# Scores of batch 2 in the fixed PSUM banks, a changed load order, and four softmax products on VectorE, in a fused attention and ELU block

## The chip, the cores and the metric

The kernel runs on one core of one Trainium2 chip. The metric is the device time of one execution in microseconds (us); the number given for a kernel is the median of several runs. Beside it one execution was profiled, and every duration of a single instruction comes from that execution.

## What is computed

For each of 8 batches a small attention block reads x (8 heads, 512 rows, 64 columns) against a state (8 heads, 32 rows, 64 columns), in both directions. The result, 512 + 32 rows of 512 columns per batch, goes through a two-layer block with ELU:

```python
scores = scale * x @ state.T;   a  = softmax(scores);   xread = a @ state
scores2 = scale * state @ x.T;  a2 = softmax(scores2);  sread = a2 @ x
h = concat([xread, sread], rows) @ w_in          # (4352, 512) @ (512, 2048)
g = where(h > 0, h, exp(min(h, 0)) - 1)          # ELU
out = g @ w_out                                  # (4352, 2048) @ (2048, 512)
```

The two weight matrices arrive as 64-bit floating point numbers, which the kernel itself turns into 32-bit ones.

## The kernel before, in words

**Algebra.** xread @ w_in = a @ (state @ w_in), so the kernel first makes M = state @ w_in for each batch (`make_m`) and then multiplies the softmax by M (`ffn1`). From batch 2 on, and for the second layer of all batches, it uses a Strassen-like scheme with seven products for eight, partly on two levels (class `Second`). That takes sums and differences of blocks, of activations and of weights, nearly all on VectorE (`sums`, `weights`, `combine`, `weight_sum`, `sum_a`), and those of M on GpSimd (`sum_m`).

**The stages.** `start` (L1150) does batches 0 and 1 together with the preparation of the weights. w_in and w_out come in 16 blocks of 1 MB (`weight_block`, L1117): blocks 0 to 7 are w_in, 8 to 15 w_out. Block 0 comes in two halves. `convert` (L1090) makes 32-bit numbers of a block by two passes on ScalarE and four on VectorE: a clamp (`tensor_scalar`), a combination (`scalar_tensor_tensor`), a shift (`tensor_scalar`) and an add, which the trace shows as a custom instruction. Three raw buffers (tile t_w) hold blocks in flight, and block n + 3 is asked for when block n is converted. Each converted block of w_in feeds `make_m` for both batches and goes back to memory (w_in_mem), where later batches fetch it. Still within `start`, the second layer of batch 0 runs (n0), and that of batch 1 (n1) begins. `ffn2_1` (L1364) finishes batch 1, on the way making the weight sums of the second level. Then the loop runs `batch(b)` for batches 2 to 7, and `states` ends with the rows of the states.

**Softmax.** `scores` (L662) writes one product into two PSUM banks. `softmax` (L760) then does, for the two halves g: a transpose from PSUM (VectorE), the maximum of 32 (VectorE), its subtraction (GpSimd), exp (ScalarE), the sum (VectorE); then a scalar step on ScalarE and a reciprocal on VectorE for both halves; then, for each half, the product with the reciprocal (L779) and a transpose into the tile that the matmuls read. The buffers are in the tile sec for batches 0 and 1 and in xr for later ones. `softmax_rows` (L746) works on the same scores for the other direction. Later `sum_a` takes four differences of the result of `softmax`.

**What sets the order.** All operations go to a planner (class `Plan`, L87), not straight to the engines. The planner knows each operation's inputs and outputs and an estimated cost, and runs a list scheduling over all of them when the program is built. TensorE takes its operations by their place in the program text, and passes over one that isn't ready or has no PSUM bank; VectorE, ScalarE and SP take the one that is due first; GpSimd keeps the order of the text. The result is a fixed order of instructions on each engine; on the chip each engine runs its own order and waits where it must. For the first 40 us of the plan idle time of TensorE is filled with matmuls whose result nobody reads (`fill`, L1587, traced as line 1590).

**PSUM banks.** There are 8. Most are given out by the planner: the one that came free first goes to the next operation that opens one, and its last user gives it back. Banks 6 and 7 are taken for good at one point (`fixed`, L559) and serve as the accumulator pb of `ffn1_chunk` from batch 2 on. Before that point they are given out like the others. In the kernel before, the point is `ident_ready` (L1137, called at L1580 and L1581 between `start` and `ffn2_1`): for each of the two banks, four 128x128 matmuls of w_out with itself, made to follow the last TensorE operation of `start`. The dictionary `kept` (L208) names, for the operation that first uses a fixed bank, that bank. `scores(2, xr)` (L1260), inside `start`, takes two ordinary banks; the scores of batches 3 to 7 (L1303) go to the fixed banks.

**Loads at the start** (L1172 to L1181), in this order by rank: the state of batch 0 (queues of SP and ScalarE), x of batch 0 in four transfers (alternately SP and ScalarE), block 0 in two (SP), the state of batch 1 (SP), x of batch 1 in four (SP), blocks 1 and 2 (SP). An x transfer moves 256-byte pieces, a block 2048-byte ones.

In the trace nearly all instructions have line 464, the one that issues every planned operation, so they are told apart by their tiles: o, s and sec for outputs and sums, t_w for raw blocks and later for weight sums, w_half and w_out for converted weights, aT for the softmax, m for M. An fp32 matmul shows as two records.

Of the kernel before, what the change touches and what calls it, by code (L numbers as in the profile page):

```python
# [86 lines left out]
class Plan:  # L87
# [108 lines left out]
    def prepare(self):  # L196
        for op in self.ops:
            op.users = []
            op.turn = self.places.get(op.number, op.number)
        for op in self.ops:  # L200
            for d in op.deps:
                d.users.append(op)
        self.opening = {}
        self.closing = {}
        for b in self.banks:
            self.opening.setdefault(b.first, []).append(b)
            self.closing.setdefault(b.last, []).append(b)
        self.kept = {b.first: b.fixed for b in self.fixed}  # L208
        self.all_banks = min([op.number for op in self.kept], default=0)

    def lag(self, a, b):
# [27 lines left out]
    def run(self, until=0.0):  # L239
# [6 lines left out]
        able = {e: [] for e in ENGINES}  # L246
        coming = {e: [] for e in ENGINES}
        banks = [(0.0, i) for i in range(self.BANKS)]
        fixed = set(self.kept.values())
        openers = sorted((op for op in self.ops if op in self.opening), key=lambda op: op.turn)  # L250
        oldest, opened = 0, set()
        in_turn = [op for op in self.ops if op.engine == POOL]
# [6 lines left out]
        def bank_time(op):  # L259

            if op in self.kept:
                return min([t for t, i in banks if i == self.kept[op]], default=None)
            need = len(self.opening[op])
            if op is not openers[oldest] and op.number > self.all_banks:
                need += self.KEPT_BANKS
            free = choice(op)
            return free[need - 1][0] if need <= len(free) else None
# [40 lines left out]
        while len(done) < len(self.ops):  # L308
# [24 lines left out]
                    after.append((holder[i], op))  # L333
                opened.add(op)
            if op in self.kept:
                banks = [b for b in banks if b[1] != self.kept[op]]
                if self.kept[op] in holder:
                    after.append((holder[self.kept[op]], op))
            while oldest < len(openers) and openers[oldest] in opened:
                oldest += 1  # L340
            if e == PE and (op.spare or op.name == "make_m"):
# [48 lines left out]
def kernel(  # L390
# [16 lines left out]
    G = 2  # L407
# [266 lines left out]
    def make_m(b, *hcs):  # L674
# [11 lines left out]
        if hcs[-1] % 2 == 0:  # L686
            plan.ops[-1].spare = st[b, "m", c][0].bank

    def m_blocks(m):
        return [m[:, g * 512 + h * 256 : g * 512 + (h + 1) * 256] for h in range(2) for g in range(2)]  # L690

# [68 lines left out]
    def softmax(b, to):  # L760
        s = st[b, "s"]
        total_t = small(b)[:, 36:68]

        def rows(g):
            return soft_t(b, g).rearrange("p (k n) -> p k n", n=NS)

        for g in range(G):
            V.transpose(out=soft_t(b, g), in_=s[g])
        for g in range(G):
            V.reduce_max(out=tops(b, g)["top_t"], in_=rows(g), axis=AX_X)  # L770
            (V if 0 & 1 and b > 1 or b in [] else Q).tensor_tensor(
                out=rows(g), in0=rows(g), in1=bc(tops(b, g)["top_t"], NS), op=ALU.subtract
            )
            A.activation(out=soft_t(b, g), in_=soft_t(b, g), func=AF.Exp, scale=scale)
            V.reduce_sum(out=tops(b, g)["total_t"], in_=rows(g), axis=AX_X)
        line(b, total_t, 1.0, eps)
        V.reciprocal(out=total_t, in_=total_t)
        for g in range(G):
            (V if 0 & 2 and b > 1 or b in [] else Q).tensor_tensor(  # L779
                out=rows(g), in0=rows(g), in1=bc(tops(b, g)["total_t"], NS), op=ALU.mult  # L780
            )
            V.transpose(out=to[:, g * 512 : (g + 1) * 512], in_=soft_t(b, g))
# [158 lines left out]
    class Second:  # L941
# [39 lines left out]
        def steps(self, out, fresh=False, base=None):  # L981

            t, s = self.t_w, self.s
            a11, a12, a22 = self.a
            x, y = bank(), bank()
            steps = []

            def step(n, ps, a, b, first, last, h, c):
                ps = ps[:, :P]
                products(  # L990
                    0.9,
                    [
                        (ps, a[:, k], b[:, k], dict(
                            start=first and k == 0, stop=last and k == FO // 4 - 1
                        ))
                        for k in range(FO // 4)
                    ],
                    "second",
                )
                o, p = (x[:, h, c * P : (c + 1) * P] for x in (out, base or out))  # L1000
                if n not in (0, 2, 3, 6):
                    p = o
                elif fresh:
                    p = None
                if p is None:
                    A.copy(out=o, in_=ps)
                else:
                    V.tensor_tensor(out=o, in0=p, in1=ps, op=ALU.add)
                if n == 1 and self.late:
                    V.tensor_tensor(out=s[4], in0=a12, in1=s[2], op=ALU.subtract)  # L1010

            for n, args in enumerate((
                (x, a11, self.b11, True, False, 0, 0),
                (y, a12, self.b21, True, True, 0, 0),
                (x, s[2], t[2], False, False, 1, 0),
                (y, s[3], t[3], True, False, 1, 1),
                (x, s[1], t[1], False, False, 1, 1),
                (y, a22, t[4], False, True, 1, 0),
                (x, s[4], self.b22, False, True, 0, 1),
            )):  # L1020
                steps.append(lambda n=n, args=args: step(n, *args))
            return steps

    second = {
# [125 lines left out]
    def start():  # L1150
# [19 lines left out]
                read_block(n + 3)  # L1170

        n = len(plan.ops)  # L1172
        load_states(0, 1, raw_s, (SP, ACT))
        load_x(0, x_halves, (SP, ACT))
        blocks[0] = weight_block(0, 2)
        load_states(1, 2, raw_s[:, 1:], (SP,))
        load_x(1, x_1)
        read_block(1)
        read_block(2)
        for k, op in enumerate(plan.ops[n:]):  # L1180
            op.rank = k  # L1181
        turn_states(raw_s[:, 0:1], kT[:, 0:1])

        def w_step(hc):
            convert_block(hc)
            w = st["w", hc] = w_half[:, hc % 3]
            c = hc // 2
            make_m(0, hc)
# [10 lines left out]
        def ffn1(b, c, tiles=range(4), split=False):  # L1199
            ffn1_plain(b, c, (g0, g_sb)[b], (a_sb, aT1)[b], e_slots, tiles, split)  # L1200

        turn_x(x_halves, ob, 1)
        scores(0, ob)
        softmax(0, a_sb)
        w_step(0)
        ffn1(0, 0, (0, 1), 0 & 1)
        turn_x(x_1, ob)
        scores(1, ob)
        softmax(1, aT1)
        ffn1(1, 0, (0, 1), 0 & 2)  # L1210
        w_step(1)
        ffn1(0, 0, (2, 3))
        ffn1(1, 0, (2, 3))
        for c in range(1, 4):
            w_step(2 * c)
# [1 line left out]
            ffn1(0, c)  # L1217
            if c < 2:
                for b in range(2):
                    softmax_rows(b)  # L1220
                    turn_state(b)
                    state_read(b, (x_halves, x_1)[b])
            ffn1(1, c)
# [33 lines left out]
        y = o.open()  # L1257
        o.product(y, o.a21, t_w[3], True)
        o.copy(y, 1, 1)
        scores(2, xr)  # L1260
        softmax(2, a_sb)
        softmax_rows(2)
        load_x(2, x_halves)
# [11 lines left out]
    def first_m(b, at=None):  # L1275
# [5 lines left out]
            sum_m(m_to[0])  # L1281
        fetch(2)
        fetch(3)

    def ffn2(o, b):

        c11, c12, c21, c22 = (o.part(i, j) for i in range(2) for j in range(2))
        nxt = b + 1 < B
        spare = spaces(m_sb[:, 1], 3)
        o.sum_1()  # L1290
        late = [plan.ops[-1]]
        if 1:
            second[1].sums(o.a11, spare + s_2[0][:1])
            steps = second[1].steps(c12, fresh=True)
            steps[0]()
        else:
# [1 line left out]
            o.product(x1, o.a11, b11, True)  # L1298
            A.copy(out=c12, in_=x1)
            steps = []  # L1300
        if nxt:
            first_m(b + 1, 1)
            scores(b + 1, xr, [f.view() for f in fixed])  # L1303
        else:
            turn_read()
        for f in steps[1:]:
            f()
        second[2].sums(o.a12, s_2[1] + spaces(a_sb))
        late.append(plan.ops[-1])
        for f in second[2].steps(c11, base=c12):  # L1310
            f()
        late.append(plan.ops[-1])
        second[4].sums(o.a22, s_2[0] + spare[:2])
        late.append(plan.ops[-1])
        for f in second[4].steps(c21, fresh=True):
            f()
        second[6].sums(o.s, s_2[1] + spaces(a_sb))
        late.append(plan.ops[-1])
        combine(o.a12, o.a12, o.s)
# [33 lines left out]
        store(b, 1, o)  # L1353
        steps = second[3].steps(c12)
        if nxt:
            make_m(b + 1, 2, 3)
            copy_m(b + 1, 1, m_to[1])
            sum_m(m_to[1])
            state_read(b + 1)
        for f in steps:  # L1360
            f()
        store(b, 0, o)
# [1 line left out]
    def ffn2_1(o, b, x1):  # L1364
# [28 lines left out]
        second[3].weights(b22)  # L1393
        steps = second[4].steps(c21)
        second[3].sums(o.a12, s_2[0])
        make_m(b + 1, 2, 3)
        copy_m(b + 1, 1, m_to[1])
        sum_m(m_to[1])
        state_read(b + 1)
        for f in steps:  # L1400
            f()
        store(b, 1, o)
# [29 lines left out]
            )  # L1432

    def batch(b):
        for hc in range(4, 7):
            fetch(hc)
        if b + 1 < B:
            load_blocks(b + 1, ob)
# [3 lines left out]
        p[0] = ffn1_chunk(b, 0, g_sb)  # L1442
        p[0][0]()
        p[1] = ffn1_chunk(b, 1, g_sb)
        p[0][1]()
        make_m(b, 4, 5)
        fetch(7)
        copy_m(b, 2, m_to[2])
        sum_m(m_to[2])
        p[1][0]()  # L1450
        p[2] = ffn1_chunk(b, 2, g_sb)
        p[1][1]()
        make_m(b, 6, 7)
        copy_m(b, 3, m_to[3])
        sum_m(m_to[3])
        if b + 1 < B:
            turn_blocks(ob, xr)
        p[2][0]()
# [118 lines left out]
        dma(out_b[rows, S:SB, cols], o.o_sb[c][:, 0, cols], kind="store_q")  # L1577

    o, x1 = start()
    ident_ready(0)  # L1580
    ident_ready(1)  # L1581
    ffn2_1(o, 1, x1)
    for b in range(2, B):
        batch(b)
# [47 lines left out]
```

## Time and profile before

| what | value |
|---|---|
| median of the 3 runs shown | 702.86 us (702.0 to 703.4) |
| the profiled execution: its own time | 702.52 us |
| the profiled execution: span of its trace | 700.6 us |
| busy in the span: TensorE, VectorE | 689.1 us (98%), 590.8 us (84%) |
| busy: ScalarE, GpSimd | 307.1 us (44%), 121.1 us (17%) |
| chain that ended last | TensorE 73%, VectorE 15%, ScalarE 5%, DMA 3% |
| granted TensorE clock, mean | 0.998 |

A busy share is a mean over stages that differ. The page's slices show VectorE at 0.8 to 1.0 from about 18 us on, ScalarE at 0.8 to 1.0 from 18 to 105 us and at 0.0 to 0.4 after that for a while, and the DMA engines at 0.7 to 0.9 for the first 70 us. A time in the trace counts from the start of the span. "A <- B" in a row reads: A is written from B; a number in brackets at the end is the idle time of the engine before the row and what ended it.

### The profile page before, as it was taken

The page shows a single profiled execution, that of the slowest core. Times are in us where ns is not written, and L with a number is a line of the kernel's source. Part 1 is how long each engine was busy: PE and PEld are TensorE (multiplying, and loading weights), DVE is VectorE, ACT ScalarE, POOL GpSimd, SP SyncE. Part 2 cuts the span into 40 slices and gives each one's busy share as a digit, 9 for nine tenths or more (in the row PEclk, how much of TensorE's full clock was granted, in tenths as well). Part 3 has the DMA queues.
Part 4 walks back from the last instruction along what each step waited for, and adds up shares of the span by engine and source line. Part 5 has one row for each costly group of instructions (what it writes and reads, how often), then busy time and mean ns, then how long its engine had stood idle before and what let it go on. Part 6 is the DMA issues. An engine that isn't in the chain of part 4 may idle for free.

```text
span 700.6 us, 14914 instructions
## 1 busy us (share of the span) xinstructions
PE 689.1 (98%) x5938; PEld 591.8 (84%) x5938; DVE 590.8 (84%) x1062; ACT 307.1 (44%) x646; POOL 121.1 (17%) x137
## 2 busy tenths in 40 slices
PE   8899999999999999999999999999999999999997
PEld 7544468889988998889888998799889988899996
DVE  4999999999849996899869995999589977999650
ACT  4998982011058023832176135713283127600530
POOL 1400000032211044101710152004410153000000
PEclk9999999999999999999999999999999999999999
DMA  9677773204264204740285026611464034100300
GB/s 221 214 265 241 267 241 56 60 31 121 75 139 161 49 2 138 195 122 1 90 227 136 1 75 167 172 41 36 131 167 122 1 98 175 59 3 31 122 8 24
DMA packets 111270, 78.57 MB, mean 112 GB/s; under 512 B 89184, under 2 KB 92768, under 8 KB 111200
## 3 DMA queue, kind: packets, MB, share of 16 engines
q1 hardware_dynamic: 108988, 77.06, 38.4%
q8 instruction: 47, 0.77, 0.5%
q10 hardware_dynamic: 2212, 0.56, 0.4%
q14 instruction: 23, 0.19, 0.1%
HBM read 61.34 MB, written 13.11 MB: 106 GB/s over the span
## 4 chain that ended last, share of the span: by engine, by line
PE 73%; DVE 15%; ACT 5%; DMA 3%; issue 3%; SPq 1%; ACTq 0%; DVEq 0%
PE ps L464 73%; DVE sec L464 3%; DVE g L464 3%; DVE w_out L464 2%; DVE t_w L464 2%; ACT sec L464 2%; DMA t_w<-in_moe_w_out_dram 1%; DVE s L464 1%; DVE w_half L464 1%; DVE xr L464 1%; ACT t_w L464 1%; SPq L464 1%; DMA g<-in_x_dram 1%; DMA xe<-in_x_dram 1%; DVE small L464 1%
## 5 line engine op out<-in xcount | busy, mean ns | idle before, releaser
L464 PE MATMUL ps<-aT,m 128*128 128x256 f32 (+1 forms) x568 | 149.6, 408 | 0.4 <-ACT m L464 0.4
L464 PEld LDWEIGHTS ps<-aT,m 128*128 128x128 f32 x568 | 104.6, 190 | 33.2 <-issue 13.6
L464 PE MATMUL ps<-w_out,g 128*128 128x128 f32 (+1 forms) x768 | 113.2, 293 | 0.7 <-DVE g L464 0.7
L464 PEld LDWEIGHTS ps<-w_out,g 128*128 128x128 f32 x768 | 102.5, 192 | 9.1 <-ACT xe L464 2.5
L464 ACT COPY o<-ps 128x128 f32<-128x128 f32 (+2 forms) x88 | 26.1, 300 | 165.2 <-PE ps L464 165.2
L464 DVE TENSOR_TENSOR o<-o,ps 128x128 f32<-128x128 f32 (+2 forms) x257 | 70.9, 286 | 27.7 <-PE ps L464 26.2
L464 POOL TENSOR_TENSOR xr<-xr,small 128x512 f32<-128x512 f32 x24 | 29.3, 1240 | 325.4 <-PE ps L464 173.7
L464 POOL TENSOR_TENSOR m<-m 128x256 f32<-128x256 f32 x72 | 62.8, 894 | 88.2 <-ACT m L464 86.7
L464 PE MATMUL ps<-sec 128*128 128x128 f32 x560 | 74.6, 276 | 0.6 <-DVE o L464 0.6
L464 PEld LDWEIGHTS ps<-sec 128*128 128x128 f32 x560 | 68.4, 192 | 2.3 <-DVE o L464 1.6
L464 PE MATMUL ps<-t_w,s 128*128 128x128 f32 (+1 forms) x432 | 65.4, 300 | 0.0
L464 PEld LDWEIGHTS ps<-t_w,s 128*128 128x128 f32 x432 | 58.5, 191 | 4.9 <-ACT m L464 0.8
L464 ACT ACTIVATE xe<-ps 128x512 f32<-128x512 f32 x96 | 54.9, 603 | 10.2 <-PE ps L464 5.7
L464 ACT COPY m<-ps 128x512 f32<-128x512 f32 (+1 forms) x56 | 27.4, 537 | 54.9 <-PE ps L464 54.9
L464 ACT COPY sec<-ps 128x512 f32<-128x512 f32 (+1 forms) x52 | 29.5, 568 | 47.0 <-PE ps L464 29.2
L464 DVE SCALAR_TENSOR_TENSOR g<-xe,ps 128x512 f32<-128x512 f32 x66 | 43.4, 681 | 4.0 <-ACT xe L464 3.8
L464 DVE TENSOR_SCALAR xe<-xe 128x512 f32<-128x512 f32 x30 | 13.7, 462 | 35.4 <-ACT xe L464 35.3
L464 ACT ACTIVATE xe<-xe 128x512 f32<-128x512 f32 x66 | 40.4, 641 | 0.7
L464 PE MATMUL ps<-aT,s 128*128 128x256 f32 x168 | 40.3, 380 | 0.0
L464 DVE TENSOR_TENSOR ps<-sec,ps 128x512 f32<-128x512 f32 (+1 forms) x52 | 34.4, 669 | 4.9 <-PE ps L464 3.3
L464 PE MATMUL ps<-sec,g 128*128 128x128 f32 (+1 forms) x300 | 37.4, 271 | 0.8 <-DMA g<-in_x_dram 0.8
L464 ACT COPY ps<-ps 128x512 f32<-128x512 f32 (+1 forms) x28 | 15.4, 551 | 50.9 <-PE ps L464 50.5
(157 smaller groups left out, 1231.8 us busy)
## 6 DMA issues: line engine op xcount, KB each, us to landing
w_half<-w_in_mem SPq DMA_DIRECT2D x54, 512.0 KB
t_w<-in_moe_w_out_dram SPq DMA_DIRECT2D x8, 1024.0 KB
t_w<-in_moe_w_in_dram SPq DMA_DIRECT2D x7, 1024.0 KB
out_dram<-o SPq DMA_DIRECT2D x14, 512.0 KB
xe<-in_x_dram SPq DMA_DIRECT2D x26, 256.0 KB
o<-in_x_dram SPq DMA_DIRECT2D x80, 64.0 KB
w_in_mem<-w_half SPq DMA_DIRECT2D x8, 512.0 KB
xr<-xr SPq DMA_DIRECT2D x96, 32.0 KB
```

The costliest lines, as they stand in the source:

```text
L464: ins = getattr(engine, name)(**named)
```

## The change

Three things change what is emitted.

1. `scores(2, xr)` is given the two fixed banks, and both calls of `ident_ready` are gone. `kept` now maps an operation to a list of fixed banks, and the planner issues such an operation only when all of its banks are free; from then on these are kept, as before.
2. The loads at the start come in the order state 0, block 0, x 0, state 1, block 1, x 1, block 2 (letters "swxtvyu"; before it was "sxwtyvu"). The queues of each stay.
3. The products at the end of `softmax` are on VectorE for batches 0 and 1 (four instructions), and stay on GpSimd for batches 2 to 7.

```diff
-        self.kept = {b.first: b.fixed for b in self.fixed}
+        self.kept = {}
+        for b in self.fixed:
+            self.kept.setdefault(b.first, []).append(b.fixed)
...
             if op in self.kept:
-                return min([t for t, i in banks if i == self.kept[op]], default=None)
+                free = [t for t, i in banks if i in self.kept[op]]
+                return max(free) if len(free) == len(self.kept[op]) else None
...
-            (V if 0 & 2 and b > 1 or b in [] else Q).tensor_tensor(
+            (V if 0 & 2 and b > 1 or b in [0, 1] else Q).tensor_tensor(
                 out=rows(g), in0=rows(g), in1=bc(tops(b, g)["total_t"], NS), op=ALU.mult
             )
...
-        load_states(0, 1, raw_s, (SP, ACT))
-        load_x(0, x_halves, (SP, ACT))
-        blocks[0] = weight_block(0, 2)
-        load_states(1, 2, raw_s[:, 1:], (SP,))
-        load_x(1, x_1)
-        read_block(1)
-        read_block(2)
+        q2 = (SP, ACT)
+        for what in 'swxtvyu':
+            if what == "s": load_states(0, 1, raw_s, q2)
+            if what == "x": load_x(0, x_halves, q2)
+            if what == "w": blocks[0] = weight_block(0, 2)
+            if what == "t": load_states(1, 2, raw_s[:, 1:], (SP,))
+            if what == "y": load_x(1, x_1)
+            if what == "v": read_block(1)
+            if what == "u": read_block(2)
...
-        scores(2, xr)
+        scores(2, xr, [f.view() for f in fixed] if 1 else None)
...
     o, x1 = start()
-    ident_ready(0)
-    ident_ready(1)
+    if not 1:
+        ident_ready(0)
+        ident_ready(1)
     ffn2_1(o, 1, x1)
```

The rest of the diff adds switches that stand at the behaviour of before: other orders of the steps of a second-level product, other places for `make_m`, `sum_1` and `scores` in later batches, a normalisation for each half of the softmax apart, and operations held behind others. None of them emits anything else.

## The prediction, as it was put on record

> **What bounds the kernel now.** I read the busy time by stretch first, with cuts where the character of the work changes. Columns: stretch and its length in us, then busy us and instruction count of TensorE, of its weight loads, of VectorE, ScalarE and GpSimd, then granted clock, DMA share, GB/s.
>
> ```profile
> 0.00:43.50 43.50, 38.84 (x362) 25.07 (x362) 33.16 (x52) 32.88 (x65) 9.99 (x15) 1.00 0.75 206
> 43.50:98.00 54.50, 54.30 (x383) 25.83 (x383) 50.28 (x66) 51.08 (x95) 0.00 (x0) 1.00 0.75 254
> 98.00:158.40 60.40, 60.40 (x292) 52.18 (x292) 60.37 (x78) 13.19 (x22) 5.86 (x4) 1.00 0.32 86
> 158.40:163.00 4.60, 3.97 (x35) 3.78 (x34) 4.60 (x9) 0.59 (x1) 0.00 (x0) 1.00 0.16 55
> 163.00:196.00 33.00, 33.00 (x392) 31.45 (x392) 26.93 (x58) 4.35 (x11) 7.93 (x8) 1.00 0.34 107
> 196.00:640.00 444.00, 442.69 (x4089) 400.88 (x4088) 387.62 (x744) 187.57 (x407) 97.36 (x110) 1.00 0.36 98
> ```
>
> From 163 on TensorE idles 1.3 us in 477. Only work or idleness ahead of 163 is in reach, and what is saved there moves the end one for one. Before 43.5 TensorE looks 89% busy, but much of that is the filler matmul of line 1590, which computes nothing:
>
> ```profile
> 0.00:45.00 45.00, 14.94 (x90) 12.86 (x90) 1.00 0.76 211
> ```
>
> With 4.7 us of idleness in 0 to 43.5 that is over 19 us in which TensorE has nothing real to do. So the start is bound by what feeds it. The chain of work that ended last says by whom: from 98 to 162.7 it is VectorE piece by piece, then TensorE alone.
>
> ```profile
> 161.29 0.60 DVE m L464
> 161.90 0.60 DVE sec L464
> 162.50 0.21 DVE o L464
> 162.70 0.04 issue
> 162.75 268.14 PE ps L464 x2592
> ```
>
> VectorE is 60.37 of 60.40 us busy there. TensorE is full as well from 43.5 on, so 162.75 is a handover: to make it earlier, VectorE's queue must get shorter (or start earlier) *and* TensorE must arrive earlier. Last, the matmuls at the handover:
>
> ```profile
> 158.38 1.95 PE L464 MATMUL ps<-w_out 128*128 128x128 f32 x16
> 160.16 1.95 PE L464 MATMUL ps<-t_w,s 128*128 128x128 f32 x16
> 162.75 1.16 PE L464 MATMUL ps<-sec 128*128 128x128 f32 x8 [0.63 <-DVE o L464]
> ```
>
> The first row is both calls of ident_ready: w_out against w_out, result never read.
>
> **A: scores in the fixed banks, no ident_ready.** Removed: 16 matmul records, 160.16 - 158.38 = 1.78 us of TensorE. They end just before a 0.63 us wait for VectorE, so they partly cover VectorE's sums (three at 0.60 from 160.62). Those sums write where batch 0's products read until 158.4, so cannot start before; s1, s2 and the add (0.60 + 0.60 + 0.28) could be done by about 160.2 if they go first, but then the work now ahead of them (0.57, 1.21 and 0.57 us from 158.26) falls due later. VectorE has gaps of only 0.16 and 0.61 us before 174. Bounds: 0 if the wait grows by what is removed, 1.78 + 0.63 = 2.4 if VectorE keeps pace. I take 0.9: between the 0.77 us of gaps and half of the removed 1.78.
> Moved: scores(2) (1.02 us at 136.54) must now have banks 6 and 7, both free. The trace has no bank numbers; the program of before puts scores in 6 and 4, and the accumulator y of batch 0 (its product starts at 129.54, its last one ends at 151.6) in 7. Taken over unchanged, scores would wait until about 151.6. TensorE does not stand still: the planner issues the other products first. Behind the scores hang softmax(2) and its 8.4 us of VectorE. Their result, with the four differences of sum_a, is done at 188.05 and wanted at 196.09: slack 8.0 against a delay of up to 15.1. Of the 20.7 us from scores to finished transposes (137.6 to 158.3) most is queueing on a full VectorE, so I take no loss; bounds -1.5 (VectorE freed for the handover: the rest of A's 2.4) to +7.1 (rigid chain).
>
> **B: first block of w_in ahead of x.** By the trace's DMA packets x (256 B each, 1 MB) moved until 7.3 us, the block (2048 B, 1 MB) from 7.3 to 10.5. Landing is seen about 1.2 us after the last packet: the halves of the block are taken by ScalarE at 10.12 and 11.62. Swapped, x is complete 3.2 us later at most. SP's queue: two issues of the block (1.58 us) now stand ahead of two of x (1.26); ScalarE's two x issues stay. Second turn of x at 8.79 becomes about 11.6, scores(0) at 10.41 about 13.2. For the block all of 3.2 would be gained if x stood still meanwhile. Here a rule of the Trainium skill speaks (DMA: Bandwidth & Descriptors, Queues, rings and completion order): each DMA engine alternates between the queues it has work for, packet by packet. The rows: 32 block packets per engine in 3.2 us are 100 ns each, x's 272 (with states) in 4.5 us 16.5 ns. By strict order the block takes 3.2 us, by the rule 32 x 116.5 ns = 3.7 us, since half of x comes on ScalarE's queue. Either way x's third row block, on SP behind the block, lands last, so scores are as late. I use 3.7: first half usable near 5.7, second near 7.5.
> VectorE's part of the conversion is 2 x (0.42 + 0.42 + 0.68 + 0.67) = 4.4 us, now between 10.8 and 22.1, then in time in which it idles. By 14.4 it would have done 0.23 + 4.4 + 1.38 (two copies of x) = 6.0 us against 4.9 in the trace: 1.1 us ahead, not 4.4, because it waits for the late x from about 12.4. ScalarE by the same count: 7.0 against 5.5, 1.5 ahead.
> Block 1 also passes the four loads of x(1): x(1) lands some 3 us later (packets until 16.0), block 1 about 4 earlier. What hides it: softmax(1) is done at 35.65 and ffn1(1,0) starts at 36.55, after 15 us behind conversions; block 1 now feeds VectorE and TensorE (make_m at 31.04 waited for it) in between. Cost 0 with that cover, up to 3 without.
>
> **C: four products on VectorE.** Nearest row: TENSOR_TENSOR 128x512 from SBUF, 0.60 us from start to start, so +2.4 us on the bounding engine. GpSimd loses four of 1.05 to 1.45 us. But VectorE was held up by these:
>
> ```profile
> 18.67 1.27 DVE L464 TENSOR_SCALAR w_half<-w_half 128x512 uint32<-128x512 uint32 x1
> ```
>
> Its twin takes 0.42; it ended just after GpSimd's product of 18.56 to 19.66. At 32.01 a 128x1024 one took 1.21 instead of 0.69. Relief 0.85 + 0.52 = 1.37, net +1.0. A rule against the change: SBUF - State Buffer, Who interferes with whom, says that a VectorE instruction with two SBUF inputs contends with a GpSimd one that reads SBUF. The new products are of that kind, and subtractions of the other batch stay on GpSimd (24.03 and 25.82, 1.05 and 1.36 us). By the rule a meeting costs up to one such duration, net +2.1 to +2.4; by the rows products of batch 0 (18.56 to 20.85) and these lie 3 us apart. Batch 1's are delayed too, so I keep +1.0, bounds +0.5 and +2.4.
>
> **The sum.** VectorE: -1.1 (B) + 1.0 (C) = -0.1. Its idle time from 20 to 98 is some 4.8 us, 3.9 of it waiting for conversions on ScalarE (w_half 2.2, w_out 0.9, t_w 0.8); ScalarE being 1.5 ahead, I take 1.0 of it back (0 to 1.5). With A's 0.9: handover 2.0 earlier. Profiled execution 702.52 (span 700.6 and 1.9 around it): 700.5. The median of the runs shown is 0.34 above it: 702.86 - 2.0 = 700.9.
>
> **Rivals.**
> *Nothing is won (0.2).* VectorE is the bound to the last: ident_ready only covered its wait, nothing is taken back from ScalarE: -0.1, 702.8. For it: 100% busy for 64 us. Against: it catches up with TensorE by 170 to 174 (gaps 0.16 and 0.61).
> *TensorE was starved more than VectorE was full (0.16).* The gaps of 12 to 14.4 are filled (B 2.5 instead of 1.1), 1.5 comes back from ScalarE, A gives its 2.4: -5.4, 697.5. For it: 19 us of fillers and idleness. Against: VectorE's tally.
> *Slower (0.14): scores(2) sits behind an occupied bank.* Place: TensorE at 136.54. It decides from 136.5 + 8.0 = 144.5 on, if the chain of softmax(2) does not shrink; rigid it costs 15.1 - 8.0 = 7.1 at 196, half rigid 3.5: 702.9 + 3.5 - 1.0 = 705.4. For it: y held bank 7 until 151.6. Against: two accumulators among eight banks miss both 6 and 7 in 15 of 28 placements, and the chain is mostly queueing.
>
> **The numbers.** My own case has 0.5, range 699.3 to 702.3. A measurement can tell about 0.2% (1.4 us) from no change: faster is below 701.45, slower above 704.27. Faster: most of my case (0.41) and the starved one: 0.57. Same: 0.09, and the first rival: 0.29. Slower 0.14. The range takes in the starved case's upper half and half of the slower one: 697.6 to 704.9.
>
> **What would show it.** Right: the block's conversion on ScalarE from 5 to 6 us, scores(0) at 13; no GpSimd product before 140 and no stretched TENSOR_SCALAR; no w_out-by-w_out matmuls; handover near 160.8, with a wait of one to two us for VectorE around it; everything after it unchanged in length. Wrong: VectorE busy under 95% between 98 and 158 (then it was not the bound), scores(2) after 144.5 with TensorE idle near 196, or a stretch after 163 that changes by more than a us, since the planner then shuffled work that I take as fixed.

## The result, and the profile after

| | before | after |
|---|---|---|
| median, same chip | 702.50 us (702.0 to 703.4) | 698.64 us (698.2 to 699.6) |
| ratio, 95% interval | | 0.9945 [0.9928, 0.9963] |
| profiled execution: own time, span | 702.52, 700.6 us | 699.62, 697.8 us |

The kernel is 3.9 us faster. The forecast was 2.0 us; direction and range held, the size was half. A second set of runs of the kernel after (after_again, below) gave 698.61 us.

Busy time by stretch, kernel after, with the cuts and columns used before:

```profile
0.00:43.50 43.50, 38.78 (x370) 26.02 (x370) 33.26 (x55) 31.26 (x63) 4.84 (x11) 1.00 0.74 199
43.50:98.00 54.50, 54.12 (x381) 25.57 (x380) 51.12 (x66) 51.89 (x97) 0.00 (x0) 1.00 0.79 259
98.00:158.40 60.40, 60.40 (x287) 53.32 (x286) 57.51 (x73) 10.36 (x13) 0.00 (x0) 1.00 0.34 86
158.40:163.00 4.60, 4.60 (x71) 2.98 (x69) 4.60 (x11) 0.00 (x0) 0.00 (x0) 1.00 0.28 114
163.00:196.00 33.00, 33.00 (x385) 31.33 (x384) 27.68 (x63) 7.74 (x21) 11.73 (x12) 1.00 0.36 111
196.00:640.00 444.00, 442.69 (x4086) 401.76 (x4071) 389.94 (x748) 186.88 (x406) 98.18 (x110) 1.00 0.36 97
```

In the third row VectorE is 57.51 of 60.40 us busy (before 60.37). In the fourth TensorE is full (before 3.97 of 4.60). The last row's TensorE figure is the same as before. The chain of work that ended last, kernel after:

```profile
62.79 0.70 DVE g L466
63.48 0.04 issue
63.53 364.62 PE ps L466 x3082
```

Before, VectorE carried this chain from 98 to 162.7. Now TensorE carries it from 63.5 to 428. The matmuls at the handover, kernel after:

```profile
157.09 1.95 PE L466 MATMUL ps<-t_w,s 128*128 128x128 f32 x16
158.96 1.09 PE L466 MATMUL ps<-xr,kT 64*32 64x512 f32 x16
159.98 1.16 PE L466 MATMUL ps<-sec 128*128 128x128 f32 x8
```

The product that waited until 162.75 starts at 159.98 and waits for nothing. The w_out-by-w_out matmuls are gone. In their place stand the scores of batch 2 (xr by kT), which were at 136.54 before. By the plan, they wait for bank 7, held until then by an accumulator of batch 0.

What their move did to VectorE is seen in its own rows. Before, batch 2's softmax began at 139.86, and these last pieces of it stood in its queue ahead of the add (o) that the handover waits for:

```profile
145.12 0.68 DVE L464 TENSOR_REDUCE small<-xr 128x16 f32<-128x512 f32 x1
...
149.44 0.67 DVE L464 TENSOR_REDUCE small<-xr 128x16 f32<-128x512 f32 x1
...
153.43 0.70 DVE L464 STREAM_TRANSPOSE aT<-xr 128x512 f32<-128x512 f32 x1
...
157.63 0.70 DVE L464 STREAM_TRANSPOSE aT<-xr 128x512 f32<-128x512 f32 x1
...
158.83 1.29 DVE L464 STREAM_TRANSPOSE xr<-xr 128x512 f32<-128x512 f32 x2
...
162.42 0.28 DVE L464 TENSOR_TENSOR o<-o,ps 128x128 f32<-128x128 f32 x1
```

VectorE, kernel after, same stretch:

```profile
147.15 0.69 DVE L466 TENSOR_TENSOR t_w<-t_w 128x512 f32<-128x512 f32 x1
150.38 0.69 DVE L466 TENSOR_TENSOR m<-m,ps 128x512 f32<-128x512 f32 x1 [2.55 <-PE ps L466]
...
158.72 0.69 DVE L466 TENSOR_TENSOR sec<-sec,s 128x512 f32<-128x512 f32 x1
159.32 0.28 DVE L466 TENSOR_TENSOR o<-o,ps 128x128 f32<-128x128 f32 x1
...
160.92 0.71 DVE L466 STREAM_TRANSPOSE xr<-ps 128x512 f32<-128x512 f32 x1
```

None of batch 2's softmax is left ahead of the add. VectorE runs out of work at 147.8 and waits 2.55 us for TensorE. The add comes at 159.32, 3.1 us earlier, and the softmax begins only behind it (160.92). The scores themselves, 1.02 us of TensorE, now stand between the last product and the handover. Without them TensorE would have waited from 158.96 for the add, which ends at 159.60, so about 0.6 us of them is hidden there (an estimate from these rows).

### The profile page after: what moved, and what is told of

Read it like the earlier page. It is cut to its first block, busy times and chain, and to the rows that moved or that the text cites. A ratio compares the mean times of both kernels' runs of the same rounds, so it can differ in the third digit from the quotient of the medians.

```text
span 697.8 us, 14901 instructions
## 1 busy us (share of the span) xinstructions
PE 686.7 (98%) x5926; PEld 590.9 (85%) x5926; DVE 589.2 (84%) x1066; ACT 305.5 (44%) x646; POOL 114.8 (16%) x133
## 4 chain that ended last, share of the span: by engine, by line
PE 87%; ACT 5%; DVE 4%; DMA 3%; issue 1%; ACTq 0%; DVEq 0%
PE ps L466 87%; ACT sec L466 2%; DVE g L466 1%; DMA xe<-in_x_dram 1%; DMA g<-in_x_dram 1%; ACT t_w L466 1%; ACT w_half L466 0%; ACT xe L466 0%; DVE ps L466 0%; DVE w_half L466 0%; ACT o L466 0%; DVE xr L466 0%; ACT m L466 0%; DVE sec L466 0%; ACTq L466 0%
## 5 line engine op out<-in xcount | busy, mean ns | idle before, releaser
L466 DVE SCALAR_TENSOR_TENSOR g<-xe,ps 128x512 f32<-128x512 f32 x66 | 43.5, 680 | 4.7 <-ACT xe L466 2.8
L466 PE MATMUL ps<-w_half,kT 64*32 64x256 f32 x1024 | 36.0, 382 | 0.3 <-DVE g L466 0.3
```

What stands on the lines that cost most here:

```text
L466: ins = getattr(engine, name)(**named)
```

## The experiments

**Theory.** The handover starts when the later of two is there: TensorE, or VectorE's add. Taking out the 16 matmul records of ident_ready (1.78 us) pays only as far as VectorE is ready earlier, and moving the scores so late that their softmax falls behind the add makes it so in the kernel after. **Rivals:** the gain comes from the earlier block and the products on VectorE (B and C); or it comes from the removed matmuls, wherever the scores stand.

All kernels are the kernel after with the edit shown, or the kernel that the text names with it. This table has their traces, in us, between three marks; handover and rest hold the same matmuls in all of them, but for the 16 records of ident_ready. "Arrival" is the first matmul of the second layer of batch 0 (t_w by s, 128x256), "handover" runs from it to the first ffn1 of batch 2 (aT by m), "rest" from there to the end. "Wait" is what TensorE waits for VectorE in the handover stretch; "scores" is when scores(2) start. The ratio is timed, against the kernel before.

| kernel | scores | arrival | handover | wait | rest | ratio, 95% |
|---|---|---|---|---|---|---|
| before | 136.5 | 122.63 | 73.46 | 0.63 | 504.5 | 1 |
| after | 159.0 | 122.55 | 70.95 | 0 | 504.3 | 0.9945 [0.9928, 0.9963] |
| after_again | 157.9 | 121.52 | 70.94 | 0 | 504.3 | 0.9949 [0.9936, 0.9963] |
| a_alone | 153.3 | 123.89 | 70.67 | 0 | 506.5 | 1.0002 [0.9994, 1.0011] |
| bc | 135.8 | 121.93 | 73.91 | 1.18 | 504.4 | 0.9989 [0.9980, 0.9997] |
| after_early | 135.0 | 121.10 | 72.66 | 1.33 | 507.9 | 1.0039 [1.0026, 1.0052] |
| late_ident | 157.3 | 122.72 | 72.62 | 0 | 505.4 | 0.9993 [0.9985, 1.0002] |
| mute_before | 139.7 | 125.82 | 74.75 | 2.13 | 504.5 | 1.0012 [0.9996, 1.0027] |
| mute_late | 156.3 | 121.64 | 71.68 | 0.78 | 505.4 | 0.9967 [0.9955, 0.9979] |
| b_alone | 136.7 | 122.83 | 72.32 | 0 | 504.6 | 0.9984 [0.9975, 0.9992] |
| c_alone | 137.3 | 123.38 | 72.74 | 0 | 504.5 | 0.9996 [0.9985, 1.0006] |
| ab | 136.8 | 122.85 | 70.68 | 0 | 504.7 | 0.9970 [0.9959, 0.9982] |
| ab_late | 158.0 | 123.39 | 70.81 | 0 | 508.5 | 1.0016 [1.0007, 1.0024] |
| a_late | 157.8 | 123.18 | 70.81 | 0 | 507.9 | 1.0026 [1.0013, 1.0039] |

One trace stands behind each row. The mark "arrival" of one and the same kernel (after, after_again) differs by 1.03 us between its two traces, its handover stretch by 0.01. So a wait of about one us in a single trace is weaker evidence than a difference between stretches or between timed ratios. In mute_before the granted clock was 0.96 in the first 43.5 us and 0.95 from 165 to 200.5, so of its row only the wait and the rest are used.

**a_alone: the banks alone, loads and products as before.**

```diff
-            (V if 0 & 2 and b > 1 or b in [0, 1] else Q).tensor_tensor(
+            (V if 0 & 2 and b > 1 or b in [] else Q).tensor_tensor(
-        for what in 'swxtvyu':
+        for what in 'sxwtyvu':
```

> Only A: scores(2) in the fixed banks, no ident_ready; loads and softmax products as before. In this program bank 7 is held by batch 0's accumulator y, so scores is issued behind its last product, at about 151 us. Theory 1 (all of the gain is A's): 3 to 4 us faster than before, ffn1 of batch 2 starts about 2.4 us earlier than the 196.09 of before. Theory 2 (B and C carry a good part, A is worth the 0.9 of the prediction): about 1 us faster, ffn1 of batch 2 near 195.2.

No gain in time, 702.45 us; neither theory's figure came. Yet its handover stretch is 2.8 us shorter than before's. The rest is 2.0 longer: the planner has put eight matmuls (16 records) of batch 3 into batch 2, and batch 3 is only 0.2 us shorter without them, with three new waits, two for VectorE and one for ScalarE, of 1.04 us together. So the part does what it should at its place, and the planner's later order takes it back.

**bc: the loads and products alone, with ident_ready.**

```diff
-        scores(2, xr, [f.view() for f in fixed] if 1 else None)
+        scores(2, xr, [f.view() for f in fixed] if 0 else None)
-    if not 1:
+    if not 0:
         ident_ready(0)
         ident_ready(1)
```

> B and C without A: the changed kernel with ident_ready and scores(2) in two ordinary banks, at about 136 us. Theory 1: within 0.5 us of before, ffn1 of batch 2 at 196.0. Theory 2: 1.5 to 3 us faster, ffn1 of batch 2 near 194. If the late x of B costs more than it gives: over 1 us slower.

701.72 us, 0.8 us faster than before (0.2 to 1.4): the first rival is out as the main cause. TensorE arrives earlier (121.9 in the mean of the six traces with both parts), and gives part of it back in a longer wait. Its matmuls at the handover:

```profile
160.35 1.06 PE L466 MATMUL ps<-t_w,s 128*128 128x128 f32 x8
162.59 1.16 PE L466 MATMUL ps<-sec 128*128 128x128 f32 x8 [1.18 <-DVE o L466]
```

From bc to after the handover stretch shrinks by 73.91 - 70.95 = 2.96 us, and that is the removed 1.78 plus this 1.18.

**after_early: the kernel after with scores(2) at their old place.** One fixed bank is another number, which is free early.

```diff
-    fixed = [Bank(plan, 6), Bank(plan, 7)]
+    fixed = [Bank(plan, 6), Bank(plan, 5)]
```

> The changed kernel, but with banks 6 and 5 as the fixed ones: both are free early, so scores(2) is issued at about 136 us as before, while ident_ready stays away. Theory 1a (the delay of scores frees VectorE at the handover, and that is what lets A give its 2.4): the wait for VectorE near 160 grows by most of the 1.8 us that is removed, 0.5 to 1.5 us faster than before, ffn1 of batch 2 at 194.8 to 195.6. Theory 1b (it is only TensorE's removed matmuls): as fast as the changed kernel, ffn1 of batch 2 at about 193.8.

Its matmuls at the handover:

```profile
158.72 1.09 PE L466 MATMUL ps<-w_half,kT 64*32 64x256 f32 x32
160.87 1.16 PE L466 MATMUL ps<-sec 128*128 128x128 f32 x8 [1.05 <-DVE o L466]
```

The wait for VectorE comes back, 1.05 us here and 0.28 further on. The stretch is 1.7 us longer than after's, so the place of the scores counts. Against bc, which has the same loads and products, it is 1.25 us shorter, so this run alone does not refute the second rival; the pair of mute kernels below bears on it more. At 704.44 us it is slower than before, which neither theory foresaw, and that is not the handover: its rest is 3.4 us longer, with new waits in batches 3 and 4.

**late_ident: bc, with scores(2) late in the text.** The matmuls stay, only the scores move.

```diff
-        scores(2, xr, [f.view() for f in fixed] if 1 else None)
-        softmax(2, a_sb)
-        softmax_rows(2)
-        load_x(2, x_halves)
...
         o.copy(x1, 0, 1)
+        scores(2, xr, [f.view() for f in fixed] if 0 else None)
+        softmax(2, a_sb)
+        softmax_rows(2)
+        load_x(2, x_halves)
```

> The changed kernel with ident_ready back and scores(2), softmax(2), its row form and the loads behind them moved to after batch 0's last product; scores in ordinary banks at about 157 us. Nothing is removed from TensorE against before. Theory 1a: only the 0.63 us wait at the handover goes, about 0.7 us faster than before, ffn1 of batch 2 at 195.4. Theory 1b, in which the delay does nothing: as before, 196.0.

701.7 us, no different from bc. The wait is gone (1.18 to 0) and the stretch 1.3 us shorter, but the rest is 1.0 longer. With the 16 records still ahead of it, TensorE itself is now the later one at the handover. The add and the matmuls behind it:

```profile
161.89 0.27 DVE L466 TENSOR_TENSOR o<-o,ps 128x128 f32<-128x128 f32 x1
```

```profile
163.16 1.16 PE L466 MATMUL ps<-sec 128*128 128x128 f32 x8
```

VectorE has its add done at 162.16, 1.0 us before TensorE comes.

**mute_before and mute_late: the 16 records not emitted.** The plan keeps its two ident_ready operations, so every engine's order is that of the kernel before, and of late_ident; the traces show it. The other switches stand as in these two kernels. Only their 16 matmul records, whose result nobody reads, are not issued.

```diff
     if not 0:
         ident_ready(0)
         ident_ready(1)
...
+        plan.ops[-1].emit = lambda: None
```

> The kernel before, planned with ident_ready and so in the same order on every engine, but its 16 matmul records are not emitted. scores(2) stays at 136 us. Theory 1a (they only covered a wait for VectorE): the wait of 0.63 us becomes 1.5 to 2.4, gain 0 to 0.9 us. Theory 1b (TensorE's time is what counts): 1.8 us faster.

> B, C and late scores with ident_ready planned but its matmuls not emitted; in the same order on every engine as the kernel with B, C, late scores and ident_ready, which was 0.5 us faster than before. Theory 1a (late scores take VectorE's softmax out of the way, so the removed matmuls count in full): no wait at the handover and 1.8 us faster than that kernel, 2.3 faster than before. If VectorE is still the bound there: under 1 us faster than that kernel.

mute_before: 702.71 us, ratio 1.0012 [0.9996, 1.0027], no gain. Its matmuls at the handover:

```profile
161.57 1.95 PE L466 MATMUL ps<-t_w,s 128*128 128x128 f32 x16
165.64 1.58 PE L466 MATMUL ps<-sec 128*128 128x128 f32 x8 [2.13 <-DVE o L466]
```

The wait grew from 0.63 to 2.13 us, 1.50 of the 1.78 removed; 0.3 is left as gain. mute_late: 700.14 us. Against late_ident the ratio falls from 0.9993 to 0.9967, some 1.8 us (0.8 to 2.9). Its matmuls at the handover, and what VectorE does ahead of its add:

```profile
161.14 1.16 PE L466 MATMUL ps<-sec 128*128 128x128 f32 x8 [0.78 <-DVE o L466]
```

```profile
157.81 1.31 DVE L466 STREAM_TRANSPOSE xr<-ps 128x512 f32<-128x512 f32 x2
159.03 1.26 DVE L466 TENSOR_REDUCE small<-ps 128x1 f32<-128x512 f32 x2
...
160.80 0.28 DVE L466 TENSOR_TENSOR o<-o,ps 128x128 f32<-128x128 f32 x1
```

Its stretch is 0.94 us shorter than late_ident's, and a wait of 0.78 is back, against the expectation of none: the scores are late, but the first 2.4 us of their softmax still stand ahead of the add. The 0.94 is what VectorE was early by in late_ident (1.0). These are the cleanest tests, since each differs from its partner (before, late_ident) in the 16 records alone, with the same order on all engines. The same records cost next to nothing where VectorE is late, and as much as VectorE is early where it is early. The two differ in B and C as well as in the place of the scores, so which of these made VectorE early is for the other runs to say.

**b_alone and c_alone.** bc with the products on GpSimd again, and bc with the loads in their old order.

```diff
 b_alone
-            (V if 0 & 2 and b > 1 or b in [0, 1] else Q).tensor_tensor(
+            (V if 0 & 2 and b > 1 or b in [] else Q).tensor_tensor(
 c_alone
-        for what in 'swxtvyu':
+        for what in 'sxwtyvu':
```

> B alone: the load order of the change, the rest as before. The kernel with B and C was 0.8 us faster than before. Theory 1 (the early block fills VectorE's idle start, and the products cost VectorE part of that again): about 1.5 us faster, handover earlier by as much. Theory 2 (the late x eats what the early block gives; C carries the gain): 0 to 0.5 us either way.

> C alone: the four products on VectorE, the rest as before. Theory 1: net +1.0 us of VectorE ahead of the handover, about 0.5 to 1 us slower. Theory 2: GpSimd's hold-ups (0.85 and 0.52 us) and the hand-offs cost more than the products: about 0.8 us faster.

The earlier block is worth 1.1 us (0.6 to 1.8) by itself; the products on VectorE make no measurable difference (0.3 us faster, interval -1.1 to +0.4), so neither theory of c_alone came true.

**after_again, ab, ab_late, a_late: is the late place needed?** ab is the kernel after without the products; ab_late is ab with the scores moved in the text as in late_ident; a_late also has the loads as before.

```diff
 ab, ab_late, a_late
-            (V if 0 & 2 and b > 1 or b in [0, 1] else Q).tensor_tensor(
+            (V if 0 & 2 and b > 1 or b in [] else Q).tensor_tensor(
```

> The changed kernel once more, beside the others of this call. If its gain is real and not the luck of one chip: 0.9930 to 0.9960 of before, about 3.5 us faster. Its start in the trace may lie up to 1.3 us off that of the first profile, since two profiles of one and the same start have lain that far apart.

> A and B without C. In this program banks 6 and 7 happen to be free early, so scores(2) stays at about 136 us. Theory 1a: the removed matmuls turn into a longer wait for VectorE, so that only B's 1.1 and at most 0.8 of A remain: 1 to 2 us faster, with a wait of 1 us or more near 160. Theory 1b (only TensorE's removed time counts): 2.9 us faster.

> A and B without C, with scores(2) and softmax(2) written after batch 0's last product, so that they come late whatever bank is free. Theory 1a (late scores and no ident_ready give about 2.5 at the handover, B about 1, C nothing): 2.5 to 3.5 us faster than before if the planner's order of the later batches costs no more than in before. If C is needed: under 2 us.

> A alone, with scores(2) and softmax(2) written after batch 0's last product. The kernel with A alone gained 2.8 us up to batch 2 and gave 2.2 back in the later batches. If that was the planner's order there, this one with another order shows the gain: 2 to 2.5 us faster than before, and stretches from batch 2 to the end of 504 to 505.5 us. If A needs B and C: no faster than before.

ab narrows the theory. Its scores stand early, at 136.8, and still the stretch is as short as after's and 1.64 us shorter than b_alone's, nearly the whole 1.78. The wait that was expected of it did not come, and it is 2.1 us faster than before. Its matmuls at the handover, and below them those of b_alone:

```profile
160.48 1.09 PE L466 MATMUL ps<-w_half,kT 64*32 64x256 f32 x32
161.50 1.16 PE L466 MATMUL ps<-sec 128*128 128x128 f32 x8
```

```profile
160.36 1.95 PE L466 MATMUL ps<-t_w,s 128*128 128x128 f32 x16
162.15 1.06 PE L466 MATMUL ps<-sec 128*128 128x128 f32 x8
```

Neither waits for VectorE. With the earlier block and without C's products in its queue, VectorE is ready early enough. So late scores are one way to have it ready and not the only one; in these traces they are needed where the earlier block and C's products are both there (bc and after_early wait, b_alone and ab do not). c_alone, with the products and the old loads, does not wait either; its TensorE arrives 1.5 us later than bc's. What A adds thus depends on the rest: timed, nothing alone (a_alone), 1.0 us (0 to 2) to B alone (b_alone to ab), 3.1 to B and C (bc to after).

ab_late and a_late have the short stretch too, 70.81, and are slower than before: their rest is 4.0 and 3.4 us longer. Where, is seen in a_late's matmuls in batch 4:

```profile
376.15 1.16 PE L466 MATMUL ps<-t_w,s 128*128 128x128 f32 x8 [0.81 <-DVE g L466]
...
379.75 1.16 PE L466 MATMUL ps<-sec,m 128*128 128x128 f32 x8 [0.53 <-DVE m L466]
...
382.88 1.16 PE L466 MATMUL ps<-w_out,m 128*128 128x128 f32 x8 [0.19 <-DVE o L466]
...
387.13 1.16 PE L466 MATMUL ps<-w_out,g 128*128 128x128 f32 x8 [0.35 <-ACT o L466]
```

The busy time between 360 and 380 of a_late, and then of after:

```profile
360.00:380.00 20.00, 18.67 (x144) 15.26 (x143) 19.22 (x31) 15.04 (x30) 3.36 (x4) 1.00 0.60 130
```

```profile
360.00:380.00 20.00, 20.00 (x159) 17.04 (x159) 19.93 (x35) 14.57 (x30) 1.57 (x3) 1.00 0.70 178
```

a_late loses 1.33 us of TensorE here, after loses none. Summed over the whole rest, the steps of TensorE that hold a wait take 3.6 us more in a_late than in after, which is all of the difference. Neither ab_late nor a_late met its expectation. Batches 3 and 4 are emitted from the same text in both; only the planner's order differs. None of these versions beats the kernel after.

## Why the prediction was right in direction and half in size

| step | predicted | measured |
|---|---|---|
| A at the handover | -0.9 (0 to -2.4) | -2.96 from bc to after; timed 0.9989 to 0.9945, -3.1 |
| B, VectorE by 14.4 us | 4.9 to 6.0 busy | 4.86 to 5.75 |
| B, ScalarE by 14.4 us | 5.5 to 7.0 busy | 5.53 to 5.47 |
| VectorE's waits for conversions, 20 to 98 | -1.0 | 3.9 to 2.6: -1.3 |
| C, net on VectorE | +1.0 | timed -0.3 (-1.1 to +0.4) |
| B and C together | -1.1 | timed -0.8 (-1.4 to -0.2) |
| rest, from 163 on | 0 | -0.2 |

**A is the mis-sized term.** The prediction had the frame right: a handover, two engines, and VectorE's chain as the limit on what A is worth. It took 0.9 because it left the scores' VectorE work where the trace of before had it, ahead of the handover. (With the scores there, mute_before shows 0.3.) It saw that scores(2) might be late, asked only whether that delays ffn1, and set "no loss". Some 7.6 us of VectorE work left the critical queue with them: all of batch 2's softmax, 3.6 us from 139.86 to 143.44 in the trace of before, and 4.0 in the pieces shown above and two reciprocals. It had this as a bound ("VectorE freed for the handover") and gave it no weight. The wait of one to two us that it expected at the handover is not there. From bc to after the term is the removed 1.78 plus the wait of 1.18. That is more than the bound of 2.4, because B and C had raised the wait from 0.63 to 1.18; the prediction added the parts up as if each had its worth apart.

**The slower rival's event came, without its price.** scores(2) start 22.4 us later, more than the 15.1 assumed. But the chain from the scores to the finished transposes shrank from 20.7 to some 15 us (160.0 to 175.3), and VectorE waits for TensorE again at 177.9 (0.99 us), which fits a queue that had just been relieved; the four differences are done at 190.9 and wanted at 193.5. Of a slack of 8.0 us, 2.6 is left, and TensorE never idles from 163 to 196. That most of the chain was queueing was the right reading. "VectorE below 95% from 98 to 158" would have told against it as the bound; it is at 95.2%, and the idle piece lies where TensorE is now the later one.

**B: right in sum, wrong in one working.** The block was to be usable at 5.7 and 7.5. ScalarE, kernel after:

```profile
7.66 0.68 ACT L466 ACTIVATE w_half<-t_w 128x512 f32<-128x512 f32 x1 [0.66 <-DMA t_w<-in_moe_w_in_dram]
...
9.42 0.69 ACT L466 ACTIVATE w_half<-t_w 128x512 f32<-128x512 f32 x1 [0.50 <-DMA t_w<-in_moe_w_in_dram]
```

Each half came 2 us late, and scores(0) stand at 14.36, not 13.2. By the trace's DMA records the block's 512 pieces took from 2.9 to 8.8 us, 5.9 us. In the kernel before they took from 7.5 to 11.0, 3.5 us and not the 3.2 that the prediction read. So the block took longer than by strict order and than the estimate from the rule (3.7; the Trainium skill, DMA: Bandwidth & Descriptors, Queues, rings and completion order). The trace shows the pieces of the two queues mixed, but in bursts: while the block moves, 1758 of the 256-byte pieces on ScalarE's queue start, 3.4 for one of the block, where one for one would be 512. ScalarE takes the second half 0.7 us after the last piece has ended, not 1.2. The page lets a queue drain a packet of several descriptors at its turn; the prediction took each piece that the trace lists for a turn. Bursts fit the page's wording better, but how many pieces make a turn is not shown here. So ScalarE was not ahead at 14.4. VectorE's waits between 20 and 98, kernel after (us in total, times, longest), shrank all the same:

```profile
DVE w_out L466 <- ACT w_out L466: 1.6, 1, 1.6
DVE w_half L466 <- ACT w_half L466: 0.6, 1, 0.6
...
DVE t_w L466 <- ACT t_w L466: 0.4, 2, 0.2
```

These three sum to 2.6 (before 2.2 + 0.9 + 0.8 = 3.9). From what, if not from ScalarE's lead, is not settled.

**C cost less than +1.0.** VectorE, kernel after:

```profile
19.18 0.98 DVE L466 TENSOR_SCALAR w_half<-w_half 128x1024 f32<-128x1024 f32 x1
...
22.85 0.63 DVE L466 TENSOR_SCALAR w_half<-w_half 128x1024 uint32<-128x1024 uint32 x1
23.39 1.28 DVE L466 TENSOR_TENSOR sec<-sec 128x512 f32<-128x512 f32 x2
```

The products take 0.64 us each, near the 0.60 costed. One hold-up of 0.35 us remains (19.18, beside GpSimd's subtraction of 17.56 to 19.61), so "no stretched TENSOR_SCALAR" did not hold, but a product stretched by GpSimd was not seen. That C is at most +0.4 alone, and a gain in the whole (ab to after_again: 700.01 to 698.61 us), was not foreseen. The table hints at where it comes: with B and without C TensorE arrives at 123.0 us in the mean of three traces (b_alone, ab, ab_late), with both at 121.9 in the mean of six. In bc the longer wait takes that back, in after nothing does. Why the products help the start is not shown.

**The rest was kept by luck.** The prediction took the order of later batches as fixed. In after, bc, b_alone, c_alone and ab, and in mute_before, whose order is held, it is (504.3 to 504.7); in the other versions it moved by 0.9 to 4.0 us, up to twice the whole forecast. Which decision of the planner tips it stays open. The changed kernel happened to fall on the good side; this risk belonged in the range.

## What to carry to other kernels

Where two engines meet at a handover, removing work from one is worth at most what the other is early (here 0.94 us of a removed 1.78 where VectorE was 1.0 early, 0.3 where it was late); so ask first what stands in the *other* engine's queue ahead of the meeting, and whether the same edit moves it behind. A delayed operation is not only a risk for its consumer: it takes its followers along out of a full queue. With a list scheduler, test an edit with the order held fixed (an operation planned but not emitted), since a new order elsewhere can be as large as the effect.

## What was not expected of the hardware

The start scatters by about a microsecond between executions. The two traces of the kernel after reach the arrival mark at 122.55 and 121.52 us. Before and a_alone, which issue the same TensorE work in the same order up to there, reach it at 122.63 and 123.89. A difference of one us at this mark can thus not be read from one trace; that B and C together bring TensorE some 1.3 us earlier rests on the means of six traces with both (121.10 to 122.72, mean 121.9) and three with neither (before, a_alone, a_late, mean 123.2). What in the start scatters is not shown.
